# One fused SSM and MLP kernel: last inverse stage split by PSUM buffer, gelu table loaded early, task order laid out anew

## Chip, cores, metric

One core of a Trainium2 chip runs the whole program. The metric is device time in microseconds (us) of one execution; lower is better. Of the engines, PE (TensorE) multiplies matrices, ACT (ScalarE), DVE (VectorE) and POOL (GpSimd) work elementwise, and SP (SyncE) mostly issues DMAs.

## What is computed

The inputs are bfloat16, with S = 2048 tokens of width D = 640. A modulation vector `silu(c) @ w_mod` gives six rows of 640. Cut to what matters:

```python
h  = layernorm(x) * (1 + ca) + sa              # x = A_q
kv = causal_conv4(k, shift_k) * v              # per channel, 4 taps
y  = irfft(rfft(kv, 2*S) * rfft(ssm_k, 2*S))[:S] + kv * ssm_D   # long convolution
x  = x + ga * (h * y)
h  = layernorm(x) * (1 + cb) + sb
g  = gelu(layernorm(h) @ w1)                   # 640 -> 640
x1 = h + shift_quarters(g) @ w2                # each quarter of channels moved by +-1, +-2 tokens
f  = x1 + gelu(layernorm(x1) @ w3) @ w4        # 640 -> 1728 -> 640
out = x + gb * f
```

The two halves hang on each other through `x`: no MLP matmul can start before some tile of `y` is done.

## The kernel before

**A list of tasks and an order written out.** The function first creates 1046 tasks with `add(engine, cost, fn, r=..., w=...)`: each is a small group of instructions for one engine, with the memory it reads and writes, from which its dependencies follow. Tasks are numbered in the order of creation. The string `ORDER` then says in which order they are emitted and on which engine: `433A` is task 433 on ACT, and the letters P, A, D, G, S stand for PE, ACT, DVE, POOL and SP. Every engine executes its own tasks in that order, so the place of a task in the string is its place in that engine's queue. `P:12` also says which PSUM buffers a PE task writes; there are four, each of two banks, and a buffer is free again once the task that copies it out has run. The costs given to `add` are not used at run time.

**The front: a long convolution by FFT as matmuls.** Tables of sines and cosines are made first (`angles`, `angles_pool` on POOL and DVE; `turns_to` and `sin_to` are ACT's Sin). Channels are processed in five blocks of 128. For both the filter (`ssm_k`) and the signal (`kv`), DVE transposes a block (L394), `stage1` (L403) multiplies by a small Fourier matrix, and `stage2_half` (L420) by a second one; `evac` (L205) copies each result out of PSUM, on ACT (L207) or DVE (L209) as ORDER says. `k_shift` (L458) makes the four-tap convolution on PE, and DVE multiplies it by `v`. Then `inverse1` takes ten parts: two DVE products with the filter's spectrum (L617), two matmul groups (L624) and two copies called z below. Between these stand `ln1_stats` (L537: mean and variance of a token tile, on DVE or, as two instructions, on ACT), the normalizations `norm` (L590, ACT or DVE), and `mod_half` (L490), which makes the modulation rows from `w_mod`.

**The last inverse stage.** `inverse2` (L649) turns z into `y` for two or three token tiles at once: 64 or 96 small matmuls of 32 rows and columns (L661) in one PE task that fills two PSUM buffers, and two copies of them. It is called for tiles 0 to 2, 3 and 4, 5 to 7, 8 to 10, 11 to 13, and 14 and 15. It needs all 20 z copies.

**From y to the MLP.** The 16 token tiles form groups: 0, 1, 2 alone, then pairs 3-4, 5-6 and so on (group 3 is 3-4, group 4 is 5-6), and 15 alone. For each group, `chain_a` makes `x + y * q` on DVE (L737, L740), with the sum beside it, and ACT the sum of squares (`square_sum`, L729); `ln_finish` (L701 on DVE or POOL, L710 on POOL, with a power instruction at L715) turns them into mean and scale. `chain_b` makes `h` (L751 or L755, L756) and the second sums, and `chain_c` normalizes again and transposes (`turn`): groups 0 to 3 on PE (L769, copied out at L775), later ones by a DMA on SP (L765). `mm_w1` multiplies by w1 (L814, and L825 for the last 32 columns of each quarter) with gelus on ACT (L820, and four small ones at L831). `mm_w2` (L868), another layernorm, `mm_w3` (L902, gelu L910) and `mm_w4` (L931) follow tile by tile, and four DMAs write each finished tile.

**Loads that wait for y.** `x_load(8, 12, y0)`, `x_load(12, NT, y0)` and the loads of w1 and w2 wait on `y0 = [("Rb", 0, D)]`, the first y tile.

**Numbers.** The change adds seven tasks, so numbers shift. Up to 431 they are the same. Some that are named below:

| what | before | after |
|---|---|---|
| gelu table load | (inside task 508) | 432 |
| inverse2 of tiles 0-2: PE; copies | 432; 433, 434 | 433, 435; 434, 436 |
| copy of w1's last columns on POOL | 441 | 443 |
| last ln1 statistics (tiles 9, 12, 13, 14, 15) | 451, 456, 457, 459, 460 | 453, 458, 459, 461, 462 |
| last inverse2 copy of tiles 11-13 | 473 | 478 |
| squares of x in tiles 0, 1, 2 | 491, 512, 532 | 498, 519, 539 |
| squares of h in tiles 0, 1, 2 | 496, 517, 537 | 503, 524, 544 |
| layernorm on POOL: h in tiles 0, 1, 2; x in group 3 | 498, 519, 539; 565 | 505, 526, 546; 572 |
| transpose of group 0, its copy | 500, 501 | 507, 508 |
| w1 gelus of groups 0 to 2 | 506, 508 to 547, 549 | 513, 515 to 554, 556 |
| w1x and w1 gelu of group 3 | 591, 589 | 598, 596 |
| first w3 matmuls | 610 | 617 |
| a w3 gelu of tile 1 | 609 | 616 |
| normalization for group 4 | 641 | 648 |
| w1 matmuls of group 4 | 649 | 656 |

Of the kernel before, what the change touches and what calls it, by code (L numbers as in the profile page):

```python
# [16 lines left out]
P = 128  # L17
# [9 lines left out]
0S 2S 19G 18D 50G 20D 21G 23D 22D 25A 4S 3S 1S 6S 27G 29D 36G 37G 28D 5S 8S 9S 11S 68G 10S 69D 24A 26G 88P:0 72G 73D 31A 30A 32D 38G 66D 89A 84P:1 85A  # L27
67D 90P:2 91A 86P:3 87D 39G 40A 102P:0 103A 100P:1 76P:2 70G 104P:0 41D 49G 101A 77A 42G 43G 105A 106P:3 107A 44A 45G 33S 47S 46S 71D 34S 12S 35S 48S
184S 181S 183S 182S 13S 14S 116P:1 92P:2 98P:0 74D 75D 117D 7S 99A 118P:3 119D 114P:0 15S 112P:1 113D 93A 110P:2 16S 115A 111A 96P:3 97A 94P:0 95D
82P:2 83A 80P:1 81A 78P:3 108P:0 51D 109A 52D 54A 56G 57D 53A 122P:2 79D 155P:1 156A 153P:0 154A 151P:3 152A 123D 157P:2 136D 120P:1 121D 173P:0 158A  # L30
55G 174A 171P:3 172A 177P:2 178D 175P:1 176A 161P:0 162D 141P:3 142A 167P:2 168D 147P:1 148A 58G 59G 163P:0 164D 165P:3 166A 137P:2 138A 145P:1 146A
230D 17S 149P:0 150A 190D 188D 126P:3 127D 139P:2 140A 60A 143P:1 199S 144A 124P:0 125D 179P:2 180A 187D 169P:3 170A 234P:1 235A 244P:2 159P:0 160A
128P:3 231D 242P:1 243A 245A 130P:0 61G 62G 186D 63G 64A 238P:1 239A 129D 131D 232D 248P:2 65G 196S 249A 246P:3 247A 185D 189G 191A 252P:0 202S 253A
134P:1 135D 132P:2 133D 236P:3 240P:1 237A 260P:0 261A 233D 250P:2 251A 241D 423D 200P:3 201A 258P:0 259D 319G 208S 192G 268P:2 269A 318S 197P:3 205S
198A 266P:1 267A 272P:2 273D 270P:3 271A 203P:0 284P:1 285A 292P:2 211S 204D 278P:3 279A 417D 276P:0 277A 342S 293D 426D 209P:1 210D 294P:2 295D 226S
290P:3 222G 291A 280P:1 281D 229G 227S 264P:0 274P:2 275D 343G 223G 265A 256P:3 262P:1 420D 206P:0 207D 257A 225G 254P:2 255D 282P:3 263A 286P:0
288P:1 287D 224G 312P:2 220S 283A 289A 212P:3 321D 320D 218G 213D 313A 328D 304P:0 305A 308P:1 316P:2 317A 217S 216G 302P:0 219S 214G 418D 228S 298P:2
215S 324P:3 325D 309A 221G 327G 326S 329D 322P:1 303A 336D 306P:0 299A 421D 323A 310P:2 296P:3 307A 334S 335G 337D 350S 297A 311A 300P:1 330P:0 301A
351G 332P:3 344D 345D 331A 314P:2 333A 315A 359G 340P:1 341A 338P:0 352D 348P:3 349A 353D 346P:2 358S 347A 360D 361D 354P:1 367G 339A 356P:3 368D 366S
369D 355A 364P:2 357A 375G 362P:0 376D 372P:1 374S 377D 401S 193A 363A 382S 370P:3 373A 384D 383G 385D 380P:0 378P:1 365A 392D 390S 391G 393D 422D  # L40
419D 424D 402P:2 427D 194D 403D 371A 388P:3 381A 379A 407S 389A 428D 386P:0 387A 416G 425D 396P:1 397A 394P:3 395A 398S 399P:0 400D 432P:12 429A 430D
434D 433A 489D 502A 510D 195G 413S 490D 491A 511D 530D 408P:3 513D 404S 405P:0 406A 531D 409A 512A 440S 492G 494D 475P:12 476A 477A 515D 532A 462P:03
463A 410S 411P:1 493G 495D 514G 435S 533D 534G 496A 497D 498G 441G 535D 464A 516D 536D 518D 499D 412A 517A 469P:20 537A 471A 519G 500P:3 538D 539G
414P:1 465G 470A 558D 449S 501D 520D 521P:3 436S 415A 507P:0 522A 443S 559D 560A 540D 541P:2 437S 542A 466P:13 431D 561D 562D 563A 564D 508A 546P:2
467D 468A 547A 548P:1 565G 448S 570D 528P:0 571D 566D 572D 567D 549A 573A 446S 568D 505P:3 506A 569A 574G 575G 447S 509G 529A 503D 523D 504D 621D 622D
472P:21 473A 526P:3 527A 623A 579D 580P:0 581A 576D 439S 543A 524D 577P:2 525D 624D 578D 625D 444S 438S 550P:3 627D 480S 551D 481S 626A 590P:0 591A
445S 482S 552A 588P:2 589A 595P:3 459D 628G 633D 629D 634D 553G 630D 631D 632A 635D 637D 636A 479S 554G 555D 556P:0 557A 592P:2 486S 596D 597A 638G
641A 639D 478S 488G 610P:3 612P:0 611A 593D 608P:2 606P:3 544D 594A 598D 613A 599G 474D 460A 603D 600D 601P:1 604P:0 609A 457D 607A 442S 454A 602A
640S 642S 651P:2 649P:3 461G 650A 450D 487S 652A 485S 605D 673P:0 667P:1 451D 545D 668A 674A 452G 582D 583D 484S 689D 690D 456A 458G 584D 585D 656P:3
692D 693D 653P:2 483S 614P:1 654D 655A 657D 694A 615D 659G 658A 671P:0 695D 660G 664D 665P:2 691A 661D 662P:3 663D 453D 669P:1 696G 701A 702D 703D  # L50
666A 735P:3 455G 672A 670A 697D 698D 699D 705G 737P:2 736A 739P:0 733P:1 616D 704A 643D 644D 645D 700A 738A 706G 709A 675P:32 710S 586D 587D 740A 755D
756D 757A 646A 707D 708S 758D 759D 717P:0 714D 761G 760A 762G 734A 763A 767D 777A 768D 711A 769D 719P:1 764D 780D 676P 718A 720A 721P:0 724P:1 647D
712D 765D 766A 677D 678D 770A 680S 771G 772G 683D 741P:32 648D 773D 774S 722D 775A 776S 785P:0 725D 726A 783P:1 713D 723A 824D 617S 825D 742P 821D
822D 827D 679S 681S 826A 743D 682S 727G 728G 731D 732S 823A 784A 828G 829A 786A 787P:3 729D 730S 833D 834D 835D 830D 831D 832A 837D 684D 685S 836A
620S 838G 790P:1 788D 789A 839D 840S 799P:0 791D 805P:3 806A 781D 841D 715D 716D 881D 749D 793G 792A 882D 842S 883A 803P:1 804A 794G 795A 796S 845P:2
846A 797D 778D 779D 884D 843P:3 844A 885D 887D 800A 801P:1 802A 618S 847P:2 848D 782D 941D 850P:3 851D 852A 886A 849A 619S 687S 798S 865P:0 866A
859P:1 860A 863P:2 807P:30 861P:1 744D 750D 753S 942D 944D 745S 853D 854G 855A 888G 893A 943A 752S 857A 889D 864A 945G 890D 856S 808P 858S 809D 891D
946A 947D 948D 950D 894D 862A 892A 895D 896A 897G 925P:2 926A 898G 751S 815D 747S 919P:3 901D 686S 920A 923P:1 899D 921P:0 949A 951G 922A 902S 900S
905P:2 906A 688S 903P:3 904A 952D 953S 956P:0 957A 954P:2 955A 907P:3 908D 910P:0 810D 958G 748S 959P:2 911D 913G 746S 816D 819S 924A 962P:1 867P:30
960D 817S 963D 813S 754S 912A 993P:2 909A 914G 812S 868P 915D 916S 917D 918S 977P:1 978A 994D 995A 996G 997G 971P:2 820S 972A 869D 998A 875D 927P:30  # L60
818S 964A 814S 811S 876D 961A 965D 966G 973P:1 967A 999S 969A 970S 870D 929D 974A 1028P:2 930D 975P:3 928P 968S 1000P:1 1001A 931S 935D 1002P:0 934S
976A 979P:13 981D 1003A 1006P:0 871S 873S 1004P:1 879S 1005A 872S 874S 936D 980P 987D 1029A 937S 933S 1026P:1 939S 1007A 877S 932S 988D 1024P:2 1025A
1032D 880S 878S 982D 983S 1008P:30 986S 991S 1027A 989S 1033D 1010D 938S 940S 1022P:2 1011D 1023A 1014S 1013S 1009P 1016D 984S 985S 1017D 1030P:13
1034D 992S 990S 1015S 1012S 1018S 1019S 1020S 1035D 1037S 1036S 1021S 1038S 1031P 1040D 1039S 1041D 1043A 1045A 1042S 1044S
"""


# [1011 lines left out]
```

## Time and profile before

| | |
|---|---|
| timed runs | 300.91, 302.41, 303.38 us; median 302.41 |
| profiled execution, span from first to last instruction | 298.7 us, median of the runs 3.7 above it |
| PE busy, of the span | 269.7 us, 90% |
| DVE, ACT, POOL busy | 218.2, 208.3, 104.8 us |
| mean granted PE clock | 0.975 |
| first matmul / first copy out of PSUM | 8.1 / 9.2 us |
| first product of inverse1 / last z copy ends | 68.4 / 96.9 us |
| first transpose / first w3 matmuls | 110.1 / 135.6 us |
| w1 of group 4 starts / last matmul starts | 141.3 / 293.7 us |

The profile is of one execution. It gives no other time for that execution than the span, so a difference is worked out on the span and carried over to the median. A row of instructions gives the line in the kernel, engine, operation, what it writes and reads, how often, the busy time in all and the mean in ns of one, and then the idle time just before them with what ended it. A wait names who waited, for whom, the total, how often and the longest. "PEld" is the load of PE's stationary operand. Busy shares are averages over stages with different limits; what an edit is worth has to be read in its own stage.

### The profile page before, as it was taken

Reading aid. Unit: us, or ns where it says so; the run is one execution under the profiler, and the core shown is the slowest. Engines: PE = TensorE matmul, PEld = TensorE weight load, DVE = VectorE, ACT = ScalarE, POOL = GpSimd, SP = SyncE. Lnnn points to the kernel's source line nnn. Section 1 sums busy time; section 2 is a strip of 40 time slices with the busy share of each in tenths; the row PEclk is TensorE's granted clock in tenths of the full one; section 3 lists DMA queues with packets and bytes.
Section 4 is the critical chain, followed back from the end, with each engine's and each line's share of the span. In section 5 each row is a group of like instructions: output and inputs, shape, how many; then the busy total and the mean of one; then the engine's idle time right before and its main releaser. Section 6 shows DMA issues by size and latency. Waiting matters only on the chain.

```text
span 298.7 us, 7890 instructions
## 1 busy us (share of the span) xinstructions
PE 269.7 (90%) x3176; PEld 208.5 (70%) x3182; DVE 218.2 (73%) x438; ACT 208.3 (70%) x341; POOL 104.8 (35%) x237
## 2 busy tenths in 40 slices
PE   0999999999989766869999999999999999999993
PEld 0666755777878436648878677787788767887871
DVE  8998999999999998898759589886361544212442
ACT  4799989999999789979868775766854705431200
POOL 5864364453216591434275426120421321100000
PEclk9999999999999859799999999999999999999999
DMA  6999999898999920563700203223113030510112
GB/s 215 275 215 184 225 137 246 225 217 221 229 253 281 280 65 2 153 203 69 273 4 0 46 5 68 56 46 60 41 40 80 5 89 6 63 43 23 29 52 60
DMA packets 58356, 35.76 MB, mean 120 GB/s; under 512 B 40032, under 2 KB 55008, under 8 KB 58320
## 3 DMA queue, kind: packets, MB, share of 16 engines
q1 hardware_dynamic: 57136, 32.01, 46.3%
q0 software_dynamic: 1088, 3.21, 4.1%
q8 instruction: 25, 0.41, 0.6%
q14 instruction: 11, 0.09, 0.1%
q10 hardware_dynamic: 96, 0.04, 0.1%
HBM read 16.31 MB, written 2.62 MB: 63 GB/s over the span
## 4 chain that ended last, share of the span: by engine, by line
PE 51%; DVE 13%; ACT 11%; DMA 10%; POOL 6%; issue 5%; SPq 2%; DVEq 0%; POOLq 0%; ACTq 0%
PE ps_w L937 17%; PE ps_w L907 14%; ACT T L207 5%; DMA Ra<-in_A_q_dram 5%; PE ps_w L873 4%; PE ps_w L818 3%; PE ps_s L427 3%; ACT RG L729 3%; DVE Rb L617 3%; PE ps_ksh L463 2%; POOL lnv L715 2%; PE ps_s L407 2%; DMA RK<-R 2%; DVE R L756 2%; PE ps_mod L493 2%
## 5 line engine op out<-in xcount | busy, mean ns | idle before, releaser
L907 PE MATMUL ps_w<-R,T 128*128 128x256 bf16 (+1 forms) x630 | 63.8, 261 | 0.7 <-DMA R<-RH 0.7
L907 PEld LDWEIGHTS <-T 128*128 128x128 bf16 x630 | 55.5, 98 | 7.9 <-issue 2.0
L937 PE MATMUL ps_w<-T,R 128*128 128x320 bf16 x416 | 59.1, 299 | 0.0
L911 ACT ACTIVATE R<-ps_w 128x1024 bf16<-128x1024 f32 (+2 forms) x36 | 28.8, 827 | 41.9 <-PE ps_w L907 41.9
L937 PEld LDWEIGHTS <-R 128*128 128x128 bf16 x416 | 40.5, 98 | 15.2
L960 DVE TENSOR_TENSOR T<-ps_w,R 128x640 bf16<-128x640 f32 x15 | 12.3, 822 | 35.4 <-PE ps_w L928 18.1
L207 ACT CAST T<-ps_s 128x1024 bf16<-128x1024 f32 x32 | 30.4, 1029 | 3.2 <-PE ps_s L407 3.1
L207 ACT CAST R<-ps_s 128x960 bf16<-128x960 f32 (+1 forms) x35 | 30.8, 964 | 1.8 <-PE ps_s L427 1.6
L407 PE MATMUL ps_s<-F1bd,Rb 128*128 128x256 bf16 x160 | 23.3, 298 | 8.7 <-DVE Rb L394 8.1
L729 ACT ACTIVATE RG<-R 128x640 bf16<-128x640 bf16 x32 | 23.5, 734 | 9.9 <-DVE R L880 6.7
L407 PEld LDWEIGHTS <-Rb 128*128 128x128 bf16 x160 | 16.7, 107 | 14.7 <-DVE Rb L394 8.6
L873 PE MATMUL ps_w<-RG,R 128*128 128x320 bf16 x160 | 23.2, 299 | 2.1 <-ACT R L820 2.1
L715 POOL TENSOR_TENSOR lnv<-lnv,mhalf 128x2 f32<-128x2 f32 (+1 forms) x29 | 22.5, 775 | 2.3
L427 PE MATMUL ps_s<-T,RG 64*128 64x160 bf16 x512 | 21.2, 230 | 0.8 <-ACT R L207 0.6
L880 DVE SCALAR_TENSOR_TENSOR R<-ps_w,R 128x640 bf16<-128x640 f32 x16 | 12.9, 819 | 11.8 <-PE ps_w L873 11.6
L427 PEld LDWEIGHTS <-RG 64*128 64x128 bf16 x512 | 17.7, 94 | 5.1 <-issue 4.6
L818 PE MATMUL ps_w<-R,RG 128*128 128x256 bf16 (+1 forms) x200 | 20.0, 259 | 1.3 <-DMA R<-RK 0.6
L873 PEld LDWEIGHTS <-R 128*128 128x128 bf16 x160 | 15.4, 98 | 8.2 <-ACT R L820 2.4
L629 PE MATMUL ps_i<-EB,Rb 128*128 128x128 bf16 x160 | 19.0, 219 | 1.5 <-DVE Rb L617 1.4
L818 PEld LDWEIGHTS <-RG 128*128 128x128 bf16 x200 | 17.1, 102 | 3.5 <-issue 2.0
L628 PE MATMUL ps_i<-EA,Rb 128*128 128x128 bf16 x160 | 19.0, 219 | 0.4 <-ACT R L207 0.3
L714 POOL TENSOR_TENSOR lnv<-stat,lnv 128x2 f32<-128x2 f32 x19 | 4.0, 212 | 40.9 <-ACT RG L729 28.7
(178 smaller groups left out, 513.5 us busy)
## 6 DMA issues: line engine op xcount, KB each, us to landing
Ra<-in_A_ssm_k_dram SPq DMA_DIRECT2D x5, 512.0 KB, 5.7
R<-in_w_mod_dram SPq DMA_DIRECT2D x6, 400.0 KB, 6.0
out_dram<-RH SPq DMA_DIRECT2D x60, 40.0 KB, 1.6
T<-in_B_w_dram SPq DMA_DIRECT2D x5, 432.0 KB, 6.2
RH<-in_w_mod_dram SPq DMA_DIRECT2D x4, 400.0 KB, 4.4
Ra<-in_A_q_dram SPq DMA_DIRECT2D x4, 320.0 KB, 6.6
RK<-R SPq DMA_DIRECT2D x5, 256.0 KB, 4.5
RK<-R POOLq DMA_DIRECT2D x5, 256.0 KB, 5.3
```

The source lines that it names most:

```text
L207: nc.scalar.copy(dst, src(ps.tile))
L407: nc.tensor.matmul(psv[:, ml, :], lhsT=xL[:, s0:s0 + P], rhs=F1r, start=True, stop=True)
L427: nc.tensor.matmul(psv[:, g, j], lhsT=Gs[p, k, 64 - 64 * cc:192 - 64 * cc], rhs=T1h[h][p, cc * 32 + k], start=(cc == 0), stop=(cc == 1), t ...
L628: nc.tensor.matmul(psv[:, w, :], lhsT=Av[:, r_, :, g_], rhs=EAf, start=True, stop=False)
L629: nc.tensor.matmul(psv[:, w, :], lhsT=Bv[:, r_, :, g_], rhs=EBf, start=False, stop=True)
L715: nc.gpsimd.tensor_tensor(rs, rs, mhalf[:, 0:n], ALU.pow)
L729: add("ACT", 0.74, lambda e: nc.scalar.activation(junk, src, ACT.Square, scale=float(D) ** -0.5, accum_out=stat[:, li, 1, t:t + 1]), r=[sk ...
L818: nc.tensor.matmul(pt[:, fb, 0:cw], lhsT=w1_sb[:, b, 160 * fb:160 * fb + P], rhs=hT[:, b, 0:cw], start=(b == 0), stop=(b == ND - 1))
L873: nc.tensor.matmul(pt[:, hf, 0:320], lhsT=gsf[:, fb, c0:c0 + P], rhs=w2_sb[:, fb, 320 * hf:320 * hf + 320], start=(fb == 0), stop=(fb == 4))
L907: nc.tensor.matmul(pt[:, fl, 0:cw], lhsT=w3_sb[:, b, fb * P:(fb + 1) * P], rhs=xT[:, b, 0:cw], start=(b == 0), stop=(b == ND - 1))
L911: nc.scalar.activation(g3[g % 2][:, f0:f0 + fn, 0:cw], ps.tile[:, 0:fn, 0:cw], ACT.Gelu_apprx_tanh)
L937: nc.tensor.matmul(bank(i, hf), lhsT=gg[:, fb, i * P:(i + 1) * P], rhs=w4_sb[:, fb, 320 * hf:320 * hf + 320], start=(fb == 0 and i == 0), ...
```

## The change

It has four parts.

1. `inverse2` makes two PE tasks of half the matmuls, each with one PSUM buffer and followed by its copy. The matmuls and copies are the same.
2. A new ACT task applies gelu to one column, so that the table is loaded there. It waits for all Sin tasks, and every gelu task waits for it.
3. The loads of w1, w2 and of x in tiles 8 to 15 no longer wait for y.
4. `ORDER` is new for all tasks. 16 PSUM copies go from ACT to DVE and 16 the other way; of the `norm` tasks 17 go from DVE to ACT and 7 back; of the `ln1_stats` five go from DVE to ACT and two back; of the small layernorm tasks at L701 eight go from POOL to DVE and three back; two roundings of angle tables (38, 42) from POOL to DVE; of the transposes' copies five go from ACT to DVE and one back; five table copies by DMA go from SP's queue to POOL's, and of the filter table's sixteen (L576) six go to SP and four to POOL.

```diff
--- before.py
+++ after.py
@@ -24,44 +24,45 @@
...
-434D 433A 489D 502A 510D 195G 413S 490D 491A 511D 530D 408P:3 513D 404S 405P:0 406A 531D 409A 512A 440S 492G 494D 475P:12 476A 477A 515D 532A 462P:03
-463A 410S 411P:1 493G 495D 514G 435S 533D 534G 496A 497D 498G 441G 535D 464A 516D 536D 518D 499D 412A 517A 469P:20 537A 471A 519G 500P:3 538D 539G
-414P:1 465G 470A 558D 449S 501D 520D 521P:3 436S 415A 507P:0 522A 443S 559D 560A 540D 541P:2 437S 542A 466P:13 431D 561D 562D 563A 564D 508A 546P:2
...
+193D 395A 399P:1 438S 427D 397A 195G 421D 444S 428D 429A 442S 433P:0 422D 413S 419D 435P:2 434A 430D 402P:3 400D 436A 431D 408P:0 403D 466P:1 432A
+517D 468G 496D 518D 409A 530A 497D 443G 520D 519A 471P:0 537D 464P:3 499D 467A 481P:2 538D 521G 465A 411P:1 522D 498A 479P:3 568D 412A 540D 500G 482A
+565D 539A 569D 472A 566D 541G 523D 570A 469P:0 501D 567A 483P:2 414P:1 571D 524A 502D 572G 480A 525D 542D 484A 475P:3 503A 504D 473P:2 543D 573A 505G
+470D 577A 526G 574D 544A 477P:0 578D 545D 474A 506D 546G 487S 579D 476A 507P:2 488S 527D 489S 575D 508A 528P:3 485S 580A 415D 514P:2 581G 486S 529D
+512P:1 576A 531D 494S 509D 515A 493S 532D 582G 533P:3 547D 491S 631D 513A 492S 510D 548P:2 534A 535P:1 490S 549D 536A 511D 555P:2 553P:3 628D 632D
+556A 583D 586D 554A 584P:1 629D 587P:2 633A 557P:3 585D 630A 634G 588D 550A 597P:2 635G 558D 595P:1 598A 560D 495G 640D 636D 641D 559A 637D 642D 596A
+561G 638D 643A 602P:1 644D 639A 562D 459A 563P:2 603D 645G 599P:3 564D 516G 646D 604A 617P:2 600D 647S 648A 605D 613P:3 601A 649S 478D 618A 615P:1
+606G 614A 453A 607D 619P:3 452D 608P:0 656P:2 455D 620A 458A 454G 610D 609D 611P:3 551D 657A 658P:0 612D 552D 680P:3 659A 696D 456D 674P:2 589A 697D
...
-        add("ACT", 0.23 + 0.00083 * n, lambda e: nc.scalar.activation(dst, xs, ACT.Sin, scale=sc), r=[r], w=[w])
+        add("ACT", 0.23 + 0.00083 * n, lambda e: nc.scalar.activation(dst, xs, ACT.Sin, scale=sc), r=[r], w=[w, ("sin", 0, 1, "s")])
...
@@ -648,24 +649,24 @@
     def inverse2(tilesA):
         n = len(tilesA)
-        pss = [Slot() for _ in range(2)]
-
-        def f(e):
-            for s in pss:
-                pst(s, name="ps_i2")
-            for a, A in enumerate(tilesA):
-                for j4 in range(4):
-                    for cg in range(4):
-                        n1 = 4 * A + cg
-                        for cpp in range(2):
-                            nc.tensor.matmul(pss[j4 // 2].tile[32 * cg:32 * cg + 32, j4 % 2, a * 160:(a + 1) * 160],
-                                             lhsT=Hs[32 * j4:32 * j4 + 32, n1, cpp, :],
-                                             rhs=Zb[32 * j4:32 * j4 + 32, cpp * 64 + n1, :, :],
-                                             start=(cpp == 0), stop=(cpp == 1), tile_position=(32 * j4, 32 * cg))
-        t1 = add("PE", 0.38 * n, f, r=[("T01", 0, 20480), ("RH", 0, 4096)], alloc=tuple(pss), act=0.2, ni=64 * n)
         yv = y_all[:, tilesA[0]:tilesA[0] + n, :].rearrange("p a (j u) -> p j a u", j=4)
         for i in range(2):
-            t2 = evac(yv[:, 2 * i:2 * i + 2], lambda t: t[:, :, 0:160 * n].rearrange("p j (a u) -> p j a u", a=n), 320 * n, pss[i],
+            ps = Slot()
+
+            def f(e, ps=ps, i=i):
+                pt = pst(ps, name="ps_i2")
+                for a, A in enumerate(tilesA):
+                    for jj in range(2):
+                        j4 = 2 * i + jj
+                        for cg in range(4):
+                            n1 = 4 * A + cg
+                            for cpp in range(2):
+                                nc.tensor.matmul(pt[32 * cg:32 * cg + 32, jj, a * 160:(a + 1) * 160],
+                                                 lhsT=Hs[32 * j4:32 * j4 + 32, n1, cpp, :],
+                                                 rhs=Zb[32 * j4:32 * j4 + 32, cpp * 64 + n1, :, :],
+                                                 start=(cpp == 0), stop=(cpp == 1), tile_position=(32 * j4, 32 * cg))
+            t1 = add("PE", 0.2 * n, f, r=[("T01", 0, 20480), ("RH", 0, 4096)], alloc=ps, act=0.2, ni=32 * n)
+            t2 = evac(yv[:, 2 * i:2 * i + 2], lambda t: t[:, :, 0:160 * n].rearrange("p j (a u) -> p j a u", a=n), 320 * n, ps,
                       [("Rb", D * tilesA[0], D * (tilesA[0] + n), "y")])
             dep(t2, t1)
@@ -789,6 +790,8 @@
             turn(hT, hTk, hn, hk, i, g < pe_c)
     E0 = 64 + S
+    add("ACT", 0.25, lambda e: nc.scalar.activation(s64[:], b_pos[:], ACT.Gelu_apprx_tanh),
+        r=[("consts", 0, 1), ("sin", 0, 1)], w=[("gelu", 0, 1), ("scol", 0, 1)])
     def gs_zero():
         def f(e):
@@ -818,7 +821,7 @@
                     nc.tensor.matmul(pt[:, fb, 0:cw], lhsT=w1_sb[:, b, 160 * fb:160 * fb + P], rhs=hT[:, b, 0:cw], start=(b == 0), stop=(b == ND - 1))
         t0 = add("PE", 2.2 if n == 2 else 1.36, f, r=[hTk, ("RG", 0, 3200)], alloc=ps, ni=40)
         t1 = add("ACT", ca(512 * n), lambda e, ps=ps: nc.scalar.activation(gsf[:, 0:4, c0:c0 + cw], ps.tile[:, :, 0:cw], ACT.Gelu_apprx_tanh),
-                 w=[("gs", t0_, t0_ + n, "gs"), ("R3", 0, 5 * GW, "gs")], use=ps)
+                 r=[("gelu", 0, 1)], w=[("gs", t0_, t0_ + n, "gs"), ("R3", 0, 5 * GW, "gs")], use=ps)
         dep(t1, t0)
         ps2 = Slot()
@@ -832,7 +835,7 @@
             for q in range(4):
                 c1 = c0 + 32 * SH[q]
                 nc.scalar.activation(gsf[32 * q:32 * q + 32, 4, c1:c1 + cw], ps.tile[32 * q:32 * q + 32, 0, 0:cw], ACT.Gelu_apprx_tanh)
-        t1 = add("ACT", 1.54 if n == 2 else 1.1, f, w=[("gx", t0_, t0_ + n + 2, "gs"), ("R3", 0, 5 * GW, "gs")], use=ps2)
+        t1 = add("ACT", 1.54 if n == 2 else 1.1, f, r=[("gelu", 0, 1)], w=[("gx", t0_, t0_ + n + 2, "gs"), ("R3", 0, 5 * GW, "gs")], use=ps2)
         dep(t1, t0)
         if CG[g][0] == 0:
             def f(e):
@@ -909,7 +912,7 @@
             def f(e, ps=ps, f0=f0, fn=fn):
                 nc.scalar.activation(g3[g % 2][:, f0:f0 + fn, 0:cw], ps.tile[:, 0:fn, 0:cw], ACT.Gelu_apprx_tanh)
-            t1 = add("ACT", ca(cw * fn), f, w=[gk3], use=ps)
+            t1 = add("ACT", ca(cw * fn), f, r=[("gelu", 0, 1)], w=[gk3], use=ps)
             dep(t1, t0)
     def mm_w4(g):
@@ -988,16 +991,15 @@
                     r=[oh], lat=1.6)
     inverse2([0, 1, 2])
-    y0 = [("Rb", 0, D)]
-    dma("SP", 800, lambda q: q.dma_start(w1_sb, B_w1.rearrange("(b p) n -> p b n", p=P)), r=y0, w=[("RG", 0, 3200)])
-    dma("SP", 700, lambda q: q.dma_start(w2_sb[:, 0:4, :], B_w2.rearrange("(g r) n -> r g n", g=4)[0:P]), r=y0, w=[("RG", 3200, 6400, "w2")])
+    dma("SP", 800, lambda q: q.dma_start(w1_sb, B_w1.rearrange("(b p) n -> p b n", p=P)), w=[("RG", 0, 3200)])
+    dma("SP", 700, lambda q: q.dma_start(w2_sb[:, 0:4, :], B_w2.rearrange("(g r) n -> r g n", g=4)[0:P]), w=[("RG", 3200, 6400, "w2")])
     for g in range(4):
-        dma("SP", 60, lambda q, g=g: q.dma_start(w2_sb[32 * g:32 * g + 32, 4, :], B_w2[160 * g + P:160 * g + 160, :]), r=y0, w=[("RG", 3200, 6400, "w2")])
+        dma("SP", 60, lambda q, g=g: q.dma_start(w2_sb[32 * g:32 * g + 32, 4, :], B_w2[160 * g + P:160 * g + 160, :]), w=[("RG", 3200, 6400, "w2")])
     add("POOL", 0.8, lambda e: nc.gpsimd.tensor_copy(w1x.rearrange("p b (g r) -> p b g r", g=4), w1_sb.rearrange("p b (g r) -> p b g r", g=4)[:, :, :, P:160]),
         r=[("RG", 0, 3200)], w=[("RG", 6400, 7040)])
-    x_load(8, 12, y0)
-    x_load(12, NT, y0)
+    x_load(8, 12)
+    x_load(12, NT)
     ln1_all((8, 10), (10, 12), (12, 14), (14, 16))
     inverse2([3, 4])
     gs_zero()
```

The lines of ORDER that are shown are those from the last z copies to the first w3 matmuls, of after, and three of before.

## The prediction

> **What bounds the kernel now.** I read the span in five stretches first, then the waits and four-microsecond stretches of the middle one, then single rows for prices. In this table of stretches the columns after the length are busy time (and instructions) of each engine.
>
> ```profile
> core 0: us, PE busy (x) PEld busy (x) DVE busy (x) ACT busy (x) POOL busy (x), PEclk, DMA share, GB/s
> 0.00:9.20 9.20, 1.08 (x6) 0.78 (x7) 8.04 (x31) 3.16 (x6) 5.80 (x16) 1.00 0.72 237
> 9.20:96.90 87.70, 83.63 (x1102) 62.98 (x1107) 85.11 (x100) 84.03 (x103) 40.37 (x61) 1.00 1.01 224
> 96.90:141.30 44.40, 33.57 (x776) 25.45 (x776) 39.88 (x106) 39.22 (x85) 22.12 (x60) 0.85 0.48 130
> 141.30:293.80 152.50, 151.25 (x1296) 119.31 (x1294) 84.32 (x202) 81.86 (x150) 36.53 (x102) 1.00 0.23 52
> 293.80:298.70 4.90, 0.19 (x1) 0.00 (x0) 0.81 (x2) 0.00 (x0) 0.00 (x0) 0.86 0.19 47
> ```
>
> Task numbers below are those after the change (up to 431 they are the same before). Three regimes. The front (first copy out of PSUM at 9.2 to last copy of the first inverse stage at 96.9) is filled by ACT and DVE alike: 96% and 97%. The back (from the w1 matmuls of group 4, 141.3) is PE alone: 1.25 us of 152.5 is not PE, so nothing can be won there. The crossing between them loses 10.8 us of PE. Who is late in it:
>
> ```profile
> PEld L661 <- issue: 6.6, 10, 2.1
> POOL lnv L714 <- ACT RG L729: 12.5, 5, 3.3
> PE ps_w L873 <- ACT R L820: 2.1, 1, 2.1
> PE ps_w1x L828 <- ACT R L834: 1.2, 1, 1.2
> ```
>
> The same middle in stretches of 4 us, with the columns of the first table:
>
> ```profile
> 104.00:108.00 4.00, 2.36 (x28) 0.85 (x27) 3.93 (x12) 3.62 (x9) 3.79 (x6) 0.50 0.68 149
> 108.00:112.00 4.00, 3.29 (x84) 2.24 (x85) 3.71 (x13) 3.37 (x6) 3.71 (x14) 0.50 0.01 4
> ```
>
> In the waits (total, times, longest) the last inverse stage (L661) stands with no releaser named, which I read as waiting for PSUM buffers; the layernorm on POOL waits for ACT's sums of squares (L729); PE waits for ACT's gelus (L820, L834). In the two stretches DVE, ACT and POOL are all at 3.4 to 3.9 of 4. So the crossing is a chain through full ACT and DVE queues, and PE waits are its result.
>
> Prices (busy, mean ns of one, after the first bar):
>
> ```profile
> L207 ACT CAST Rb<-ps_i 128x960 bf16<-128x960 f32 x5 | 4.7, 955 | 0.4 <-PE ps_i L661 0.3
> L209 DVE CAST Rb<-ps_i 128x960 bf16<-128x960 f32 x3 | 3.4, 1148 | 0.0
> L592 ACT ACTIVATE RQ<-Ra,nb,rs 128x640 bf16<-128x640 bf16 x6 | 5.4, 923 | 1.1 <-DVE R L737 1.1
> L594 DVE TENSOR_SCALAR RQ<-Ra,rs,nb 128x640 bf16<-128x640 bf16 x10 | 4.4, 436 | 1.5 <-POOL nb L562 1.5
> L834 ACT ACT_TABLE_LOAD x1 | 1.3, 1283 | 0.0
> 115.56 1.28 ACT L834 ACT_TABLE_LOAD   x1
> 118.01 0.44 PE L828 MATMUL ps_w1x<-R,RG 128*128 128x128 bf16 x5 [1.24 <-ACT R L834]
> ```
>
> **What the skill says.** "ScalarE: Activation LUTs", section "What ACT_TABLE_LOAD costs": about 1283 ns plus a drain of about 1380. The trace has the 1283, and the gelu after it starts at 116.85, without the drain; I take 1.28. "TensorE: Matmul & The Clock Gate", section "What's actually happening": an idle PE falls to half clock and needs sustained work to leave it. Agrees: 0.50 in 104 to 112. "GPSIMD Engine Reference", section "Key points": POOL shares SBUF interfaces with DVE and contends. Agrees: the one-column power (L715) takes 1.08 to 1.12 us at 103.5 to 108 and 0.55 at 111.0. "TensorE: Matmul & The Clock Gate", section "Architectural detail: the array is 16× 32×32, not 1× 128×128": ACT and DVE take instructions strictly in order, so a place in ORDER is a place in a queue; the trace shows each engine in ORDER's order.
>
> **Part 1, the split.** The same 512 matmuls and copies. A half now needs one free PSUM buffer, not two, so the 6.6 us of L661 waits can go. That is PE time off the path: the y copies behind them sit in an ACT queue that is full anyway. Worth 0 to 1.5 us, contained in part 5.
>
> **Part 2, the gelu table.** The 1.28 leave the place at 115.56, where PE waited 1.24. 1.28 plus an activation of some 0.3 (nearest row: the 0.27 of a 32x128 gelu) come between the first y copies and the first sum of squares. Its new edge to the sines costs nothing: the last sine (64) is long over. Total ACT work rises 0.3; in part 5.
>
> **Part 3, loads freed of y.** The x loads of tiles 8 to 15, w1 and w2 no longer wait for the first y. SP issues two x loads just past mod load 196 (at 49 us before), the rest between the last swaps and 413. Behind them stands 413, whose mod matmul 414 comes before the transposes on PE. At about 280 GB/s (the page's peak slices), 4 MB issued from about 88 are in at about 103, needed at 110: nothing. w1 is needed by POOL's copy 443, now ahead of the first layernorm; issued about 92 and 8.4 to land, it is there at 100.4. If loads came 3 us later, that copy would hold POOL and all first layernorms: up to +2.
>
> **Part 4, the front.** I summed ACT's queue up to the last z copy (397 or 395) with the trace's durations, 0.085 taken off each for overlap. Before: 86 copies 79.8, sines 4.6, two ln1 statistics 2.8, two mod copies 0.7: 87.9, ended at 96.9, so 9.0 idle, 7.4 of it before the first copies. After: 85 copies (of a larger mix) 80.0, sines 4.6, three statistics 4.6 (188 and 190 come from DVE, 193 goes), three mod copies 1.0, one normalization 0.8: 91.1. DVE's sum to its last product falls from 87.2 to 85.2. The start is no earlier: 38 (rounding for an angle table, 1.95 on POOL, some 0.55 on DVE by the 0.57 of L306 there) and 23 now stand before the first transpose 69, so it ends near 8.7 instead of 8.06; ACT fills that with sines it did later. So ACT's 7.4 stay, and the last z copy comes between 91.1 + 7.4 = 98.5 and 91.1 + 9.0 = 100.1, plus up to 1 if it waits more. I take 99.7: **+2.8**. The cover for this would be idle ACT time, of which only 1.6 us exists after the start.
>
> **Part 5, the crossing**, by hand from the last z copy as zero, along ACT's queue: 429 to 0.9, y copies 434 and 436 to 2.75, gelu table 4.3, 409 and 530 5.6, squares of tile 1 at 6.3, two y copies, tile 0 at 8.35, tile 2 at 10.15 (before: tiles 0, 1, 2 at 5.1, 6.5, 8.4). Then y copies and tiles 3, 4 stand between; second squares of tiles 1, 0, 2 at 13.3, 15.6, 18.0 (before 9.8, 12.0, 12.8); two y copies; first transpose copy 508 ends 20.4 (before 14.5). So the first tiles come about 5 us later. But then nothing is left of tables or y copies (one, 478, on DVE later): gelus run 515 to 554 from 21.9 to 28.0, w1x gelu of group 3 30.3 to 31.8 (before 31.5 to 33.0), its w1 gelu to 33.6 (34.9); w2 of tile 2 at 35, w3 about 36.5 (38.75). Statistics 459 (1.6) delay 648 to 38.2; before, its w1 started 4.0 after that task ended (SP's transposes lie between), so group 4's w1 starts about 42.3 against 44.4: **-2.0**. Bounds: ACT without any wait, -4.5; POOL powers at 1.1 and one late copy each, +1.
>
> **Part 6, the back.** 14 us of ACT work more in all (norms from DVE), in a stretch with 70 of 152 idle; statistics 453, 458, 462, 461 stand in front of w3 gelus whose PSUM buffers PE needs (616 is evacuated late). PE cannot gain over 1.2; I take +0.5, bounds -0.5 and +2.5. The end (4.9 us) keeps its order.
>
> **Sum.** 2.8 - 2.0 + 0.5 = +1.3: span 298.7 to 300.0. The profile gives no own time beyond its span; the median lies 3.7 above it, held constant: 303.7. A change under 1% is about what a measurement here cannot tell from none.
>
> **Rivals.** *A, the crossing pays in full:* ACT's surplus in the front fills existing waits as far as it can (+1.6), with single-buffer halves ACT never stands in the crossing (-4.5), and the back gives 0.5: 302.4 - 3.4 = 299.0. For it: 10.8 us of idle PE and the L661 waits. Against it: 96% ACT in the front.
> *B, slower: the late first squares.* Part 5's 5 us are not made up, because POOL takes the pairs in listed order (572, 505, 526, 546) and each waits for ACT; w1 then starts on a cold PE. Front +3.3, crossing +1.5, back +1: 308.2. It decides from the point where group 4's w1 comes more than 44.4 after the last z copy. For it: L714's 12.5 us for L729. Against: gelu work afterwards is shorter.
> That PE is released by the split but nothing follows is my forecast's own part 1.
>
> **Numbers.** Forecast 0.40 (own range 301.5 to 306), A 0.28, B 0.32. A is faster by over 1% in three of four, B slower in seven of eight, the forecast slower in one of five: faster 0.21, within 1% 0.43, slower 0.36. Range 298.0 to 309.0: A and B with the loads' +2 left partly out.
>
> **What would show it.** Last z copy at 98.5 to 100.5 with ACT over 96% busy (part 4); gelu table near 102.5 and PE without L661 waits of 1.5 us (1, 2); first transposes near 119, w3 near 136, group 4's w1 near 142 (5); PE over 98.5% from there (6). Wrong if the last z copy ends before 98, or PE loses over 2 us after 142.

## Result and profile after

Timed beside each other, 20 runs each: 302.19 us before, 303.50 us after (302.3 to 306.73); the ratio is 1.0057, 95% interval 1.0037 to 1.0077. A second set (22 runs after, in the experiments) gave 1.0029, interval 1.0006 to 1.0051. So the change costs 0.3 to 0.6%, 0.9 to 1.7 us (by the two intervals together, 0.1 to 0.8%). The forecast was 303.7 us. Times of one kernel spread over up to 5 us, and a profile shows one execution of them.

The span of the profiled execution is 301.7 us, and its own time 303.47: 1.8 us lie outside the span. The stretches of the changed kernel, cut at the same events as in the table of before (last z copy 101.74, w1 of group 4 144.5), with the same columns:

```profile
core 0: us, PE busy (x) PEld busy (x) DVE busy (x) ACT busy (x) POOL busy (x), PEclk, DMA share, GB/s
0.00:9.20 9.20, 0.00 (x0) 0.00 (x0) 8.09 (x32) 3.78 (x6) 5.55 (x16) 1.00 0.71 235
9.20:101.74 92.54, 85.21 (x1112) 63.46 (x1113) 84.68 (x94) 85.69 (x107) 41.25 (x67) 1.00 1.02 215
101.74:144.50 42.76, 34.20 (x767) 27.17 (x766) 37.72 (x102) 39.42 (x84) 21.17 (x56) 0.76 0.60 176
144.50:296.80 152.30, 152.19 (x1305) 119.82 (x1303) 82.97 (x209) 90.49 (x164) 38.43 (x98) 1.00 0.18 39
296.80:301.70 4.90, 0.56 (x4) 0.09 (x1) 0.81 (x2) 0.00 (x0) 0.00 (x0) 0.96 0.20 50
```

Against the 87.7, 44.4, 152.5 and 4.9 us of before, the front is 4.8 longer, the crossing 1.6 shorter, the back 0.2 shorter, the end unchanged. In the front ACT has 85.69 us of work in 92.54, 93% and no longer 96%: the longer front holds waits as well as work. In the back PE misses 0.11 us of 152.3, where 1.25 of 152.5 were missing before; its work there is 0.9 longer.

The waits of the changed kernel (who, for whom, total, times, longest):

```profile
PEld L664 <- issue: 8.6, 8, 2.7
PE ps_mod L494 <- DMA RK<-in_w_mod_dram: 1.9, 2, 1.1
PE ps_w L876 <- ACT R L823: 1.4, 1, 1.4
POOL RG L998 <- DMA RG<-in_B_w_dram: 3.5, 1, 3.5
```

and POOL's own within the crossing alone:

```profile
POOL lnv L715 <- ACT RG L730: 4.5, 5, 1.7
```

The last inverse stage (L664, which was L661) waits more than before, 8.6 us for 6.6. The POOL waits for sums of squares fell from 12.5 to 4.5, and PE's wait in w1x for a gelu (L828 before, 1.2) is gone. Two waits are new, and both are for loads: PE for the modulation weights, and POOL's copy 443 (L998) for w1.

**What the last inverse stage waits for.** The prediction read its waits as waits for PSUM buffers. The timeline of PE before speaks against that:

```profile
99.50 0.39 PE L661 MATMUL ps_i<-T,RH 32*32 32x160 bf16 x28
101.45 0.65 PE L661 MATMUL ps_i<-T,RH 32*32 32x160 bf16 x36 [1.56 <-issue]
102.42 1.34 PE L661 MATMUL ps_i<-T,RH 32*32 32x160 bf16 x64 [0.32 <-ACT modv L508]
105.48 0.94 PE L661 MATMUL ps_i<-T,RH 32*32 32x160 bf16 x23
108.20 1.42 PE L661 MATMUL ps_i<-T,RH 32*32 32x160 bf16 x73 [1.78 <-issue]
```

A task has 64 or 96 of these matmuls. PE stands still after 28 of 64 and after 23 of 96, in the middle of tasks whose buffers it already has. The wait in front of a whole task, 0.32 us, does name a releaser, a copy. "issue" means that the engine waited for nothing that the profile shows. After the change the same happens, and at one place ACT is seen waiting for it:

```profile
104.40 0.48 PE L664 MATMUL ps_i<-T,RH 32*32 32x160 bf16 x28
107.27 2.23 PE L664 MATMUL ps_i<-T,RH 32*32 32x160 bf16 x116 [2.39 <-issue]
109.00 0.69 ACT L208 CAST Rb<-ps_i 128x640 bf16<-128x640 f32 x1 [0.55 <-PE ps_i L664]
```

The list of DMA queues has a line for instructions, in both kernels:

```profile
q8 instruction: 25, 0.41, 0.6%
```

These are 25 transfers of 16 KB, against 6358 and 6364 records of matmuls and weight loads, so about one per 255. Three of them start at 104.83, 111.25 and 118.31 us in the changed kernel, and PE goes on at 107.27, 113.74 and 120.65. In the 14 profiles of this case there are 31 waits "issue" of over 0.6 us at this line, and every one ends 2.3 to 2.9 us after the start of such a transfer, while the last copy out of PSUM ended anywhere from 0.1 to 3.1 us before. So it is likely that PE waits there for its own instructions, which these small matmuls use up quickly (48 of them, with as many weight loads, take 0.74 us elsewhere in these traces). No run tests it.

The middle in stretches of 4 us, columns as in the first table:

```profile
104.00:108.00 4.00, 1.61 (x80) 1.10 (x80) 3.83 (x13) 3.96 (x8) 0.43 (x3) 0.84 1.10 309
108.00:112.00 4.00, 3.33 (x101) 1.88 (x81) 3.96 (x10) 2.89 (x7) 3.67 (x5) 0.50 0.76 199
112.00:116.00 4.00, 2.26 (x122) 1.93 (x122) 3.90 (x13) 3.94 (x11) 2.45 (x5) 0.50 0.03 8
```

DVE is as full as it was, and so is ACT but for 1.1 us of waiting for PE in the second row. From 108 to 124 PE's clock is 0.50 in every such stretch (before, 104 to 112). The timeline of ACT around the gelu table (start, us, operation):

```profile
103.42 0.96 ACT L208 CAST Rb<-ps_i 128x960 bf16<-128x960 f32 x1
104.40 1.28 ACT L793 ACT_TABLE_LOAD   x1
105.69 0.20 ACT L793 ACTIVATE s<-b_pos 128x1 f32<-128x1 f32 x1
105.80 0.41 ACT L509 CAST modv<-ps_mod 128x320 bf16<-128x320 f32 x1
```

The load stands between the first y copies and everything else, 1.28 us and no drain behind it: 0.01 us later the first gelu starts.

### The profile page after: what moved, and what is told of

The parts are those of the page before. It is cut to its first block, busy times and chain, and to the rows that moved or that the text cites. A ratio compares the mean times of both kernels' runs of the same rounds, so it can differ in the third digit from the quotient of the medians.

```text
span 301.7 us, 7927 instructions
## 1 busy us (share of the span) xinstructions
PE 272.2 (90%) x3182; PEld 210.5 (70%) x3182; DVE 214.3 (71%) x436; ACT 219.4 (73%) x359; POOL 106.4 (35%) x234
## 4 chain that ended last, share of the span: by engine, by line
PE 60%; DMA 12%; ACT 11%; DVE 6%; issue 4%; SPq 4%; POOL 1%; DVEq 0%; POOLq 0%; ACTq 0%
PE ps_w L910 19%; PE ps_w L940 19%; ACT T L208 7%; PE ps_w L876 6%; DMA RK<-in_w_mod_dram 6%; PE ps_w L821 5%; PE ps_i L664 3%; SPq L234 3%; DMA RG<-RG 2%; DMA R<-in_A_k_dram 2%; DMA RK<-R 2%; PE ps_s L408 2%; PE ps_mod L494 2%; PE ps_ksh L464 1%; PE ps_w1x L831 1%
## 5 line engine op out<-in xcount | busy, mean ns | idle before, releaser
L208 ACT CAST T<-ps_s 128x1024 bf16<-128x1024 f32 x33 | 31.4, 1045 | 1.0 <-PE ps_s L408 0.9
L208 ACT CAST R<-ps_s 128x960 bf16<-128x960 f32 (+1 forms) x32 | 28.9, 983 | 4.2 <-PE ps_s L428 3.9
L408 PEld LDWEIGHTS <-Rb 128*128 128x128 bf16 x160 | 16.5, 105 | 15.6 <-DVE Rb L395 9.6
L821 PE MATMUL ps_w<-R,RG 128*128 128x256 bf16 (+1 forms) x200 | 20.8, 267 | 0.0
L208 ACT CAST T<-ps_i 128x1024 bf16<-128x1024 f32 x20 | 19.5, 1181 | 0.0
L464 PE MATMUL ps_ksh<-R,RQ 128*128 128x512 bf16 x80 | 19.0, 380 | 0.5 <-ACT T L208 0.3
L821 PEld LDWEIGHTS <-RG 128*128 128x128 bf16 x200 | 18.1, 107 | 1.7 <-issue 0.2
```

Source lines behind the costliest of these rows:

```text
L208: nc.scalar.copy(dst, src(ps.tile))
L408: nc.tensor.matmul(psv[:, ml, :], lhsT=xL[:, s0:s0 + P], rhs=F1r, start=True, stop=True)
L464: nc.tensor.matmul(pt[:, i, :], lhsT=diagw[:, b, jj, :], rhs=kT[:, b, c0:c0 + 512], start=(jj == 0), stop=(jj == 3))
L821: nc.tensor.matmul(pt[:, fb, 0:cw], lhsT=w1_sb[:, b, 160 * fb:160 * fb + P], rhs=hT[:, b, 0:cw], start=(b == 0), stop=(b == ND - 1))
```

## Experiments

Ratios are to the kernel before, timed beside each experiment (302.16, 302.46, 302.21 and 301.95 us in the four sets). "z" is the end of the last z copy, "crossing" the time from there to the start of group 4's w1.

**Two more profiles, of before and of after.** Both kernels unchanged.

> The kernel before, once more, for a second profile: the first had a span of 298.7 us, while the timed runs of the changed kernel lie 1.8 above their spans, which puts the median before at a span of 300.4. Theory (the first profile of before was a fast execution): span 300.0 to 301.0, last z copy at 97.3 to 98.6, w1 of group 4 44 to 45 us later. Rival (the profile is typical, and the offset is larger for before): span 298.5 to 299.3, last z copy at 96.7 to 97.1.

> The changed kernel once more, timed beside the other two and with a second profile. One profile gave the front 101.7 us and the crossing 42.8; the run with the late gelu table, whose front is the same, gave 103.1. Theory: ratio to before 1.004 to 1.007 again, last z copy between 101 and 103.2, 42.4 to 43.2 from there to group 4's w1, 157.2 from there to the end. Rival (the first result was high by chance, and what the late gelu table gained, 0.5%, was no gain): ratio 1.000 to 1.003.

The second profile of before, in its stretches:

```profile
0.00:9.20 9.20, 1.08 (x6) 0.78 (x7) 8.04 (x31) 3.16 (x6) 5.75 (x15) 1.00 0.71 236
9.20:98.72 89.52, 84.31 (x1108) 62.45 (x1107) 85.02 (x100) 84.29 (x103) 40.44 (x62) 1.00 1.00 218
98.72:143.20 44.48, 33.54 (x776) 25.53 (x776) 39.96 (x106) 39.26 (x85) 22.11 (x61) 0.85 0.47 131
```

Its span was 301.2 at 302.85 us. The crossing is the same to 0.1 us; the front took 1.9 more with the same work on ACT (84.29 against 84.03). The theory holds in kind: the first profile of before had been a short execution, by a little more even than expected (span up to 301.0, z up to 98.6). The second of after: span 301.6, z 102.1, crossing 41.7 (below what was expected), rest 157.8; ratio 1.0029, which lies in the rival's range, so the first figure was probably somewhat high. Means of the two profiles each:

| | front to z | crossing | rest | span |
|---|---|---|---|---|
| before | 96.9, 98.7: 97.8 | 44.5, 44.5: 44.5 | 157.4, 158.0: 157.7 | 300.0 |
| after | 101.7, 102.1: 101.9 | 42.8, 41.7: 42.3 | 157.2, 157.8: 157.5 | 301.7 |
| difference | +4.1 | -2.2 | -0.2 | +1.7 |

The mark between crossing and rest favours the new order by some 0.5 us: before, the small w1x product of group 4 stands ahead of its w1 (140.88 us), after it stands behind (147.01).

**Part 1 alone: the split in the order of before.** Each word of the last inverse stage becomes two. The code is that of the change, so the loads are free of y here too, at their old places in the order.

```diff
- 432P:12
+ 433P:1 435P:2
```

> Part 1 alone: the order of before, with each last inverse task as two adjacent halves of one PSUM buffer each; the gelu table task stands directly before the first gelu, where the table was loaded anyway. Theory (the split frees PE, but the y copies sit in a full ACT queue): 301.9 to 302.6 us against 302.2 before, last z copy at 96.9, group 4's w1 at 141 to 142, and the waits of the last inverse stage for buffers stay at several us in all. Rival (the waits for two buffers were on the path): 300.7 us or less, group 4's w1 at 139.8 or earlier, waits of that stage under 2 us.

302.54 us, ratio 1.001 (0.9989 to 1.0032); z 97.3, group 4's w1 at 142.5, and PE's waits in that stage:

```profile
PEld L664 <- issue: 7.3, 8, 3.4
```

The split does nothing to the time that these runs show, and the waits did not even become shorter. The theory holds in both (group 4's w1 came 0.5 us later than it said). Its reason for the waits, buffers, does not: in this profile too the long ones, 1.5 and 3.1 us, end 2.6 and 2.8 us after the start of an instruction transfer.

**Part 2 undone: the gelu table late.** Task 432 directly before 515, in the changed kernel and later in the best order known by then.

> The changed kernel with the gelu table task directly before the first gelu (515) instead of behind the first y copies. Theory (ACT is full all through the crossing, so 1.5 us move from one place of one queue to another): first squares 1.5 us earlier, first gelus as before, time 303.1 to 303.9, the same within 0.4. Rival (the load stood on the path at the gelus, and stands off it now): 304.5 to 305.0. Second rival (it is the early squares that are on the path): 302.0 to 302.6.

> The old front with the new rest, with the gelu table task directly before the first gelu. Theory (the table stands in the way of the first squares, 0.5% as in the changed kernel): ratio to before 0.987 to 0.991 against 0.9936. Rival (ACT's queue is full either way and the place of 1.5 us in it makes no difference): 0.992 to 0.995.

303.11 us, ratio 1.001 (0.9986 to 1.0034), against 1.0057 and 1.0029 for the changed kernel; the crossing was 43.0. By itself the ratio left the second rival open. In the other order it was 0.9941 (0.9914 to 0.9968) late against 0.9936 (0.9915 to 0.9957) early: no difference. So the theory of the first run stands for the time: 1.5 us of ACT change their place in a full queue. Of the first squares only those of tile 1 came earlier, by 0.8 us and not 1.5.

**Part 3 in part undone: three x loads late.** On SP's queue:

```diff
- 199S 196S 450S 447S 318S 202S 451S 208S 205S 211S
+ 199S 196S 318S 202S 208S 205S 211S
...
- 442S 413S 487S
+ 442S 413S 450S 447S 451S 487S
```

> The changed kernel with three of its freed x loads (450, 447, 451; 160 KB each, issued at 51 to 55 us between modulation loads) put behind the last modulation load 413. Theory (these loads delay the modulation weights and hold PE, and through it ACT and DVE): PE's waits for the modulation weights in the front fall from 1.9 us to under 0.5, the last z copy ends at 99.7 to 100.7 instead of 101.7, and the time falls from 303.5 to 301.8 to 302.7. Rival (ACT's surplus of work alone sets the end of the front): the waits go, but the last z copy moves by less than 0.5 and the time stays at 303.2 to 303.8.

301.99 us, ratio 0.9996 (0.9970 to 1.0022). DMA issues from 50 to 70 us (KB each, median us to landing), of the changed kernel first and then of this one:

```profile
RH<-in_w_mod_dram SPq DMA_DIRECT2D x4, 400.0 KB, 7.4
RK<-in_w_mod_dram SPq DMA_DIRECT2D x2, 400.0 KB, 8.4
Ra<-in_A_q_dram SPq DMA_DIRECT2D x3, 160.0 KB, 7.8
```

```profile
RH<-in_w_mod_dram SPq DMA_DIRECT2D x3, 400.0 KB, 4.6
RK<-in_w_mod_dram SPq DMA_DIRECT2D x2, 400.0 KB, 5.3
```

In the changed kernel PE waits for these weights (1.9 us in the front, in the waits above) and then starts the second-stage matmuls behind the product; with the loads late it has no such wait in the front:

```profile
63.13 0.85 PE L494 MATMUL ps_mod<-RK,silu_w 128*128 128x320 bf16 x5 [0.78 <-DMA RK<-in_w_mod_dram]
63.92 1.42 PE L428 MATMUL ps_s<-T,RG 64*128 64x160 bf16 x36
```

ACT's waits from 40 us to the last z copies, in the same order:

```profile
ACT R L208 <- PE ps_s L428: 2.8, 4, 1.4
```

```profile
ACT R L208 <- PE ps_s L428: 0.7, 3, 0.3
```

And the stretch from 60 us to the last z copy:

```profile
60.00:101.74 41.74, 36.55 (x627) 31.31 (x625) 37.31 (x47) 38.94 (x46) 14.72 (x28) 1.00 0.98 235
```

```profile
60.00:99.63 39.63, 36.16 (x624) 31.00 (x622) 37.05 (x46) 38.86 (x46) 13.80 (x28) 1.00 0.95 236
```

ACT has the same 38.9 us of work, in 2.1 us less. With the three loads of 160 KB among them the modulation weights took some 3 us longer to land; PE takes its tasks in order, so the modulation product held the second-stage matmuls behind it, and ACT waited for those. The theory holds. The pattern repeats: of the profiles with the statistics on ACT, the four with the loads early have waits of PE for these weights of 1.9 to 3.2 us and z at 101.7 to 103.1, the two with them late have none and z at 99.6 and 100.6. In time it is 0.3 to 0.6%, 1.0 to 1.8 us, by the two figures of the changed kernel; the interval here overlaps that of the second. The profile with late loads is of an execution of 300.91 us, 1.1 below the median of its runs.

**Part 4: ACT's statistics.** 188 and 190 on DVE, alone and with the late loads.

```diff
- 188A 190A
+ 188D 190D
```

> The changed kernel with the ln1 statistics 188 and 190 on DVE, as before, at the same places in the order: ACT loses 3.2 us of work in the front, DVE gains 2.2. Theory (ACT's work sets the end of the front, DVE has 6 us idle in 40 to 80): last z copy 1.5 to 2.5 us earlier than 101.7, time 301.3 to 302.3. Rival (waits set the end of the front: loads and PE): ACT only idles more, last z copy within 0.6 of 101.7, time 303.0 to 303.8.

> Both edits at once: the three x loads behind 413, and the statistics 188 and 190 on DVE. Alone the loads gave 302.0, the statistics 303.15 (their ACT time turned into idle time: 14.4 us idle before the last z copy instead of 12.3). Theory (ACT's surplus counts once the waits for the loads are gone): more than the sum, last z copy at 97.5 to 98.6 and 300.3 to 301.2 us. Rival (places in the order, not ACT's sum, set the front: DVE's statistics stand in front of copies and transposes that PE needs): no more than the loads alone, 301.7 to 302.4.

303.15 us, ratio 1.003 (1.0008 to 1.0052), z 101.3; with the late loads 303.59, 1.0037 (1.0013 to 1.0061), z 101.5. In the first, ACT's work up to z fell from 89.5 to 86.9 us, and its idle time rose from 12.3 to 14.4. What it waits for from 40 to 60 us, in the changed kernel and then here:

```profile
ACT T L208 <- PE ps_s L408: 0.6, 2, 0.3
```

```profile
ACT T L208 <- PE ps_s L408: 4.5, 6, 2.1
```

ACT waits for first-stage matmuls, whose inputs are DVE's transposes, and the statistics now stand in DVE's queue among these. So the theory that taking ACT's surplus away shortens the front fell in both runs. But the statistics came to DVE ahead of the transposes; another place on DVE was not tried. The rival of the second also expected too much: the pair was not as good as the loads alone. Its profile shows 4.3 us of the same wait (0.4 with the loads alone) and a crossing of 44.7 instead of 42.3, in which PE stands 8.8 us at L664 instead of 4.5; it is of an execution 2.0 us above the median, so how much of this is typical stays open.

**Part 4: the start.** The first transpose and its angle table ahead of 38, as before; the second time, which is shown, with 24 and 26 early as well, and the late loads. 23 goes ahead of 22, in a part of the order that is not shown.

```diff
- 28D 3S 6S 38D 5S 31A 23D 8S 39G 68D 24A 69D 30A 26G
+ 28D 3S 6S 68D 69D 38D 5S 24A 31A 8S 26G 39G 30A
```

> The changed kernel with the start as before: the angle table 23 ahead of 22, and the first transpose (68, 69) ahead of 38 and the rest. Theory (ACT waits 1.5 us longer for the first matmul and is never idle long enough afterwards to make it up): first matmul at 8.1 to 8.6 instead of 9.6, last z copy 0.7 to 1.5 us earlier, time 302.0 to 302.8 against 303.5. Rival (what is late at the start is made up by later slack, or the moved tables come late for the second stage at 27 us): last z copy within 0.4, time 303.1 to 303.9.

> The changed kernel with the three x loads behind 413 and the start as before, this time with 24 and 26 (the small Fourier matrix that the first matmul needs) early as well; in the run before, 26 stood behind 38 and 39 on POOL and the first matmul came at 10.9 us. Theory (the 1.5 us at the start are carried to the end of the front): first matmul at 8.3 to 8.8, last z copy 0.7 to 1.4 us earlier than with the loads alone, ratio to before 0.995 to 0.998 against 0.9996. Rival (a later start is made up: in the run before it was later by 1.3 us and the time no longer): ratio 0.999 to 1.001.

In the first, 26 (the small Fourier matrix of the first matmul) stood behind 38 and 39, so PE waited longer than before the edit:

```profile
PE ps_s L408 <- POOL F1bd L334: 10.9, 1, 10.9
```

So this run did not do what it was made for. Although the start was later by 1.3 us, the ratio was 1.0026 (1.0001 to 1.0050), no worse than the changed kernel's; z came at 102.8. In the second, the first matmul came at 8.4 us, z at 100.6 (99.6 without it), and the ratio was 1.0004 (0.9976 to 1.0033), against 0.9996 without it. So the earlier start did not bring an earlier end of the front, as the rival had it. The intervals are some 0.3% to each side, so the times alone could hide a good part of a microsecond. Where it is made up was not tried.

**Front and crossing apart.** The order of before (and SP's loads as there) up to 433, then the new order.

> The changed code with the order of before up to the first half of the last inverse stage, SP's loads in the order of before too (now without the wait for y), and from there the new order. Theory (front and crossing add up: the new crossing takes 42.8 us from the last z copy to group 4's w1 instead of 44.5): last z copy at 96.9, group 4's w1 at 139.4 to 140.2, time 300.2 to 301.0. Rival (the new crossing is only shorter because its front came later and had done loads and statistics): 44.0 us or more between the two, time 301.8 or more.

300.65 us, ratio 0.9936 (0.9915 to 0.9957). z came at 98.4 and 97.6 in this run's profile and in that of its copy with the late table, the crossing took 43.9 and 43.5. The time is as the theory said, so the cost of the front can be left out and a gain stays; but of the crossing's 2.2 us only 0.8 were left, close to what the rival said. The timeline of PE after the last z copies names the place:

```profile
98.47 0.74 PE L664 MATMUL ps_i<-T,RH 32*32 32x160 bf16 x48 [0.44 <-ACT T L208]
99.14 0.85 PE L494 MATMUL ps_mod<-R,silu_w 128*128 128x320 bf16 x5
100.51 0.74 PE L664 MATMUL ps_i<-T,RH 32*32 32x160 bf16 x48 [0.51 <-ACT modv L509]
```

A modulation product (405) stood between the two halves, its buffer was the second half's, and ACT in front of its copy sat idle. The product itself ran at once, so its weights were not late:

```profile
100.03 0.43 ACT L509 CAST modv<-ps_mod 128x320 bf16<-128x320 f32 x1 [1.61 <-PE ps_mod L494]
```

**The product behind the second half, in another buffer.**

```diff
- 405P:2 406A 195G 429A 435P:2 434A 430D 436A
+ 195G 429A 435P:2 405P:3 434A 430D 436A 406A
```

> The old front with the new rest, with the modulation product 405 (and its copy 406 on ACT) behind the second half of the last inverse stage instead of between its two halves, in PSUM buffer 3 instead of 2. There, the first y copies ended 3.7 and 4.6 us after the last z copy, in the changed kernel 1.8 and 2.6. Theory (the product, whose weights land late, holds PE and its buffer, and y copies and all that follows on ACT wait): y copies 1.5 us earlier, 42.0 to 43.0 us from the last z copy to group 4's w1 instead of 43.5 to 43.9, ratio to before 0.988 to 0.991. Rival (the 1.5 us are idle ACT time that is filled elsewhere, or the delay only moves to 406): ratio 0.992 to 0.995.

298.61 us, ratio 0.9878 (0.9845 to 0.9912), span 296.7; z 96.8, crossing 42.0. Both halves run back to back, and ACT's y copies follow the last z copy with one normalization between:

```profile
96.84 1.22 PE L664 MATMUL ps_i<-T,RH 32*32 32x160 bf16 x96 [0.44 <-ACT T L208]
97.99 1.53 PE L494 MATMUL ps_mod<-R,silu_w 128*128 128x320 bf16 x10
```

```profile
97.61 1.82 ACT L208 CAST Rb<-ps_i 128x960 bf16<-128x960 f32 x2
99.32 0.45 ACT L509 CAST modv<-ps_mod 128x320 bf16<-128x320 f32 x1
```

The theory holds but for the late weights (place and buffer of the product were changed together), and this version beats both kernels, the one before by 1.2%.

## Why the prediction was right, and where its terms were not

The outline was the predicted one: a longer front against a shorter crossing, PE alone from there. The sum was +1.3 us; the medians moved by 1.3, the ratios by 0.9 to 1.7. That the number fits so well is in part luck: the front came 1.3 longer than said, the back 0.7 and the crossing 0.2 shorter, and half of the front's cost came by a way that the forecast had put at nothing. The terms, against the means of two profiles each:

- **Part 1, the split (nothing by itself):** right in time, wrong in the waits. "The 6.6 us of L661 waits can go" did not happen: they are 7.3 with the split alone and 8.6 in the changed kernel. The reading behind it, PSUM buffers, failed: PE stops in the middle of tasks. "PE time off the path" is doubtful too. In the seven profiles that have the new crossing with the table early and the new front, the waits "issue" of over 0.6 us at L664 are 2.7 to 8.8 us in all and the crossing 41.0 to 44.7, and the two rise together (correlation 0.97, about 0.6 us per us). That is not a test, and a cause common to both is not excluded.
- **Part 2, the table (0.3 us of ACT):** right. It ended 4.2 us after the last z copy (4.3 predicted); late or early, the ratio is the same in the better order. "ScalarE: Activation LUTs", section "What ACT_TABLE_LOAD costs", adds a drain to the 1283 ns; here too the gelu followed at once.
- **Part 3, the freed loads (nothing):** this step failed. I asked whether 413 and w1 would come late and passed over the modulation loads among which the three x loads went: "SP issues two x loads just past mod load 196". These and a third cost 2.1 us of the front in one pair of profiles, and 1.0 to 1.8 us by the ratios. The bound that I did give, w1 late for POOL's copy 443, came true as a wait (3.5 us) but cost nothing that shows: tile 1's layernorm on POOL started 0.7 us after its squares.
- **Part 4, the front (+2.8):** +4.1. Of this, ACT's work up to z is 89.4 against 87.3 (+2.1, where I had +3.2) and its idle time 12.5 against 10.5 (+2.0, where I had -0.4). The mis-sized term is the idle time: I kept ACT's waits of before for an order that has others. The sign that I had given, ACT over 96% busy with a last z copy by 100.5, was wrong on both counts. The runs show in its place the waits for loads, which are some 2 of the 4.1. Whether ACT's extra work makes the other 2 is not shown: the run that took it away brought other waits. Moving the statistics back to DVE did not help, so the sum of one queue was no bound that could be bought back in this way.
- **Part 5, the crossing (-2.0):** -2.2. From the last z copy in the first profile of after: squares of tiles 1, 0, 2 at 5.9, 8.6, 10.9 (6.3, 8.35, 10.15 predicted); second squares 14.2, 16.4, 18.7 (13.3, 15.6, 18.0); first transpose copy 21.3 (20.4); w1x gelu of group 3 31.7 to 33.2 (30.3 to 31.8); first w3 38.4 (36.5); group 4's w1 42.8 (42.3). But for the first squares of tile 1, the walk along ACT's queue ran 0.2 to 1.9 us ahead. The late first squares, rival B's ground, were made up as the forecast had it; B decides at 44.4.
- **Part 6, the back (+0.5):** -0.2. PE lost 0.1 us from 144.5 on (0.6 in the second profile). The statistics in front of the w3 gelus cost nothing that shows.
- **The base:** I took the first profile (298.7) as typical and held 3.7 us between span and median. Some 1.65 to 1.9 are outside the span (all kernels here); the rest was that this execution was a short one, most of it in the front. Since the change was added to the median, the error did not enter the forecast.

Rival A said 299.0 of the change as it stands and was wrong by 4.5 us. That the new crossing, freed of the new front and of one product in its way, gives 298.6 does not bear it out: the crossing won 2.5 us there, where A had 4.5.

## What to carry over

When a load is freed of a wait, look at what it is then issued in front of and which engine waits for that: three loads of 160 KB among weights that PE needed soon cost 1 to 2 us here. A wait without a named releaser is not yet a wait for a buffer: see whether it falls at the start of a task or inside it. A sum over one engine's queue bounds a stage only if its waits are counted anew for the new order, and a cut in that sum can come back as waiting. When two stages of a new order move in opposite directions, run each with the other's old order: the part worth keeping, with one product moved, was 1.2% faster, while the change as a whole was 0.3 to 0.6% slower.

## What the runs showed that I had not expected

Two profiles of the kernel before differed by 2.5 us of span, 1.9 of it before the last z copy, where the DMA share is 1.0; the crossing agreed to 0.1 us. The two of the changed kernel agreed to 0.1 us in span, but their crossings differed by 1.1. One profile is not enough to place a stage within a microsecond.

The mean duration of a copy does not give its rate. Runs of z copies on ACT, in the timelines of before and after:

```profile
87.64 4.64 ACT L207 CAST T<-ps_i 128x1024 bf16<-128x1024 f32 x5
```

```profile
89.24 5.75 ACT L208 CAST T<-ps_i 128x1024 bf16<-128x1024 f32 x6
```

The mean records are 1076 ns before and 1181 after. But the rows are shorter than five and six times that, since each copy starts before the record of the one ahead has ended: one starts every 0.90 us in both kernels. So the copies did not become slower.
